# A new instruction order for the five engines in a block of sliding-window attention and gMLP on one core

## Chip, cores and metric

The kernel runs on one core of a Trainium2 chip. The time is device microseconds of one execution; the kernel before has a median of 277.32 us over three runs (277.1 to 277.49). One further execution of it was recorded by the profiler; it took 277.13 us.

## What is computed

One block on x of 2048 rows and 448 columns: attention over a window of 256 keys, then a gMLP whose spatial product mixes all 2048 rows, both behind a layer norm that is scaled and shifted by values from a conditioning vector c.

```python
mod = (silu(c) @ w_mod).reshape(1, 6, 1, 448)         # sa, ca, ga, sb, cb, gb
h = layernorm(x) * (1 + ca) + sa
q, k, v = split(h @ wqkv)                             # 16 heads of 28
p = softmax(where(0 <= i - j < 256, q @ k.T * 28**-0.5, -1e9))
x = x + ga * ((p @ v) @ wo)
h = layernorm(x) * (1 + cb) + sb
z = gelu(h @ w_in)                                    # 448 -> 1792
z1, z2 = z[:, :896], layernorm(z[:, 896:])
g = w_sp @ z2 + b_sp[:, None]                         # 2048 x 2048 times 2048 x 896
x = x + gb * ((z1 * g) @ w_out)
```

## The kernel before

**Tiles.** The 2048 rows are 16 tiles t0 to t15 of 128 rows, and four blocks tb0 to tb3 of four tiles. Everything stays in the on-chip memory; only x, the weights, two small rows of modulation values (`modrow`) and the result pass through DRAM.

**First norm and q, k, v.** DVE takes the statistics of x (L580, L583), POOL the inverse root (L585, L586), and DVE (L593) or POOL (L599) writes the normed tile `xn`. For tb0 and tb1 PE transposes it (L624, L712) and the modulation is applied as the banks are emptied into `hT` (L634/L635, L720/L722); for tb2 and tb3 a transposing DMA does it (L481, `hT<-xn`) and the modulation follows in place (L705/L707). The modulation values come from small products L537 with `w_mod`, one for each of four chunks of 128 rows. PE then forms q and k in eight groups g0 to g7 of four matmuls a block (L644 for tb0, L735 after it), which ACT or DVE copies out (L740/L741 q, L745/L746 k), and v by tile (L777; L781/L782). One more layout of q, `QBD`, is written by four small DMAs a block (L678).

**Attention.** Each tile j has two halves a and b of eight heads. I call the score group S(j)a, S(j)b. From tile 2 on such a group is 36 small matmuls (L879) into PSUM banks 0 to 3 and one matmul of 512 columns from `QBD` (L888, "Se") into bank 5. ACT takes the exponential of the four banks in one instruction of 128x2048 and of bank 5 in one of 128x512 (both L840). There is one set of banks 0 to 3, so S of a half cannot start until the exponential of the half before has read it. This gives a **ring**: score, exponential, next score; there are 28 such halves. DVE applies the masks (L895), PE multiplies with v (L922, bank 4), DVE divides (L936 reciprocal, L938) into `o_sb`, a transposing DMA (L481, `hT<-o_sb`) turns it, and PE multiplies with wo (L947). I call the last two oT(j) and mo(j). DVE adds x (L952), and the second norm and transposing DMA of the tile follow (`hT<-xn` again, from `xn2`), then its modulation (L970 ACT, L972 DVE or POOL).

**gMLP.** The two halves of w_in (L1032, L1053) are followed by gelu on ACT (L1039, L1061) and the norm of z on DVE (L1044). After that PE runs the spatial product L1077 in groups of 16 matmuls of 512 columns, DVE adds the bias (L1081), POOL multiplies with z1 (L1084), PE multiplies with w_out (L1094, L1102), DVE adds x (L1105, L1119) and SP sends the result. w_out is scaled by POOL (L963) before.

**Fillers.** At the start PE has little to do; matmuls on a tile of zeros (L550, one of 512 columns each) are put in there. The program defines 40 of them and emits those that the order names: 17.

**What sets the order.** Nothing decides at run time. A list of 1226 operations with their dependences is built, and the string `ORDER` (lines 22 to 74) names each as `n.engine.slot`: operation number, engine (p PE, a ACT, v DVE, g POOL, s SP for DMA issues) and the PSUM banks or buffers that it takes. Each engine executes its operations in the order in which the string names them, and waits on semaphores where one depends on another engine, so an engine whose next operation is not ready holds all behind it. `LAND_*` (lines 393 to 397) and `land=` (lines 424, 425) are expected landing times of loads; they go into `op.end`, which sorts only the order in which an instruction's several waits are written (`items = sorted(want.items(), key=lambda x: -x[1][1].end)`).

Of the kernel before, what the change touches and what calls it, by code (L numbers as in the profile page):

```python
# [19 lines left out]
57.v 0.a 3.a 26.v 1.s 2.s 4.s 34.g 23.v 24.v 27.v 43.a 5.s 35.g 6.s 36.g 58.p.0 59.p.0 60.p.0 44.p.0 7.s 139.v 40.g 50.a 32.g 8.s 137.v 37.g 140.v 9.s  # L20
25.v 138.v 143.v 141.g 38.g 10.s 145.v 142.g 146.v 28.v 144.v 45.a 11.s 46.a 147.g 149.v.0 148.g 151.v.1 12.s 61.p.0 62.p.0 63.p.0 64.p.0 65.p.0
66.p.0 67.p.0 68.p.0 69.p.0 70.p.0 150.p.2.3 152.p 13.s 153.v.2 52.p.1 53.p 71.p.0 54.p 155.v.3 14.s 55.p 154.p 29.v 156.p 15.s 16.s 56.v 133.a 157.v
21.s 134.v 158.a 159.v 72.p.0 73.p.0 74.p.0 191.p.4 17.s 171.p.5 135.g 186.p.6 160.v 18.s 161.p.0 136.a 172.p 162.p 192.p 49.g 176.p.1 163.p 47.a
177.p 196.p.2 166.p.3 42.g 193.p 41.g 164.p 213.v 167.p 165.a 173.p 178.p 215.v 168.p 48.a 174.p 51.v 179.p 214.v 217.v 197.p 169.p 175.a 219.v 187.p
198.p 170.a 199.p 39.v 181.p.0 180.a 188.p 218.v 220.v 194.p 216.v 200.v 189.p 221.g 195.a 182.p 222.g 183.p 30.v 184.p 190.a 374.p.0 185.v 205.p.1
375.a.0 229.g 225.g 211.s 227.g 223.g 122.p.0 228.v.0 226.g.1 212.s 201.p.6 224.v.2 19.s 230.g.3 123.v 206.a 380.p.0 125.s 202.v 231.p.0 381.a.1 210.s
234.p.1 232.v 124.s 235.v 399.p.0 233.a 203.p.6 209.s 236.v 400.a.2 269.v 251.p.0 31.v 271.v 401.a 243.p.1 376.v 265.v 126.s 252.a 406.p.0 267.v 127.s
407.a.3 241.p.0 244.v 270.v 266.v 268.v 239.p.1 272.v 204.v 408.a 273.g 274.g 242.v 377.p.0 240.a 402.v 426.p.0 378.v 237.p.0 279.g 427.a.4.0 382.v
277.g 319.v 33.g 428.p.0 281.g 280.v.0 379.p 263.p.1 275.g 320.v 282.v.1 285.s 276.g.2 321.v 238.a 434.p.0 384.v 278.g.3 247.p.0 264.v 435.a.5.1 283.s
409.v 383.p 129.g 249.p.1 248.v 284.s 322.v 411.v 385.p 429.a 455.p.0 131.g 250.v 245.p.0 456.a.6.2 386.v 323.v 286.s 132.g 387.v.0 207.p.1 325.v  # L30
403.p.0 256.s 457.p.0 246.v 208.a 463.p.0 458.a 253.s 404.v 259.p.1 464.a.0.3 438.v 255.s 439.v 405.p 410.p 388.s 261.p.0 430.v 431.v 412.p 262.a
484.p.0 254.s 413.v 287.v 436.p.0 485.a.1.4 414.v.1 257.p.0 459.v 432.p.0 288.v 433.p 290.v 440.p 258.v 437.a 492.p.0 289.v 260.a 465.p.0 489.v 441.p
493.a.2.0 295.p.0 326.v 460.v 442.v 305.p.1 488.v 466.a 324.v 443.v.2 327.g 513.p.0 296.a 328.g 468.v 444.s 515.p.0 514.a.3.1 461.p.0 467.v 462.p
291.p.0 335.g 497.v 415.s 130.g 306.v 469.p 516.a 521.p.0 292.v 329.g 470.p 522.a.4.2 331.g 336.v.0 297.p.1 333.g 332.v.1 330.g.2 471.v 472.v.0
486.p.0 445.p.0 496.v 473.s 487.a 542.p.0 298.a 446.v 494.p.0 543.a.5.3 490.p.0 447.v 22.s 389.p.1 334.v.3 337.s 526.v 491.p 303.p.0 390.v 495.a 517.v
338.s 550.p.0 304.a 525.v 301.p.1 551.a.6.4 546.v 339.s 391.v 293.p.0 518.v 498.p 302.a 340.s 554.v 552.p.0 499.p 294.a 571.p.0 500.v 553.a 501.v.2
474.p.1 310.s 572.a.0.0 307.s 299.p.0 475.v 309.s 476.v 523.p.0 519.p.0 502.s 524.a 555.v 520.p 300.a 579.p.0 448.v 547.v 317.p.1 580.a.1.1 341.g
308.s 477.v 527.p 576.v 528.p 311.p.0 478.g 342.v 479.g 392.v 318.a 529.v 344.v 573.p.0 530.v.1 480.g 600.p.0 574.a 343.g 312.v 416.p.1 531.s
601.a.2.2 449.g 584.v 544.p.0 503.p.0 450.g 417.v 20.s 393.g 575.v 548.p.0 545.a 608.p.0 504.v 549.p 418.v 556.p 609.a.3.3 505.v 315.p.1 419.v 420.g
557.p 451.g 394.g 349.p.0 558.v 605.v 316.a 421.g 581.p.0 583.v 629.p.0 582.a 559.v.0 345.p.1 630.a.4.4 506.v 604.v 560.s 577.p.0 507.g 346.v 395.g  # L40
578.p 452.g.0 602.p.0 585.p 350.a 508.g 633.v 637.p.0 603.a 586.p 509.g 396.v.1 638.a.5.0 351.p.1 481.g.2 453.v 422.g 587.v 454.s 612.v 610.p.0
347.p.0 588.v.2 352.a 642.v 658.p.0 611.a 589.s 606.p.0 348.v 659.a.6.1 561.p.1 613.v 128.s 660.p.0 397.v 641.v 607.p 398.s 614.p 423.g.0 562.v 661.a
666.p.0 482.v 615.p 662.v 667.a.0.2 313.p.0 355.s 634.v 483.s 631.p.0 563.v 532.p.1 616.v 564.v 314.a 617.v.1 565.g 687.p.0 510.g.1 632.a 533.v
# [223 lines left out]
def bass_adaLN_cond__sliding_block__mixer_gmlp__prompt_kernel(  # L267
# [13 lines left out]
    S, D, H, DH = 2048, 448, 16, 28  # L281
# [910 lines left out]
```

## Time and profile before

| | value |
|---|---|
| median of 3 runs | 277.32 us |
| profiled execution | 277.13 us |
| span in its profile, first to last instruction | 275.4 us |
| outside the span | 1.73 us |
| PE busy in the span | 265.9 us (97%) |
| DVE, ACT, POOL busy | 162.9, 128.2, 111.6 us |
| first exponential (of tile 0) starts | 19.49 us |
| first exponential of the ring, S(2)a, starts | 28.94 us |
| last score of the ring, S(15)b, starts | 104.36 us |
| first spatial product starts | 154.28 us |
| last product's result starts to be added | 272.16 us |

Times within the profile are counted from the start of the span. An engine's busy time counts each matmul from its start to its modelled end, and as matmuls overlap in the pipeline, a group of several takes longer by its row than the distance to the next group.

### The profile page before, as it was taken

What the parts mean: (1) busy time and instruction counts of PE and PEld (TensorE: products, weight loads), DVE (VectorE), ACT (ScalarE), POOL (GpSimd) and SP (SyncE); (2) the same over time, 40 slices, a digit from 0 to 9 for tenths busy, and PEclk for the clock granted to TensorE, in tenths of its full rate; (3) what the DMA queues carried; (4) which work ended last, traced back from release to release, by engine and by line L of the source; (5) the groups of instructions that cost most, each with busy time, mean ns of one, the idle gap of its engine ahead of it and who ended that gap; (6) DMA issues with size and microseconds to landing.
All of it is one profiled execution on the core that took longest, in us unless ns stands there. A gap on an engine that the chain in (4) does not pass through costs nothing.

```text
span 275.4 us, 7324 instructions
## 1 busy us (share of the span) xinstructions
PE 265.9 (97%) x3174; PEld 139.3 (51%) x3196; DVE 162.9 (59%) x365; ACT 128.2 (47%) x152; POOL 111.6 (41%) x185
## 2 busy tenths in 40 slices
PE   8898999998999999999999999999999999999995
PEld 2544566465667575544444444444444444454452
DVE  7578999997899899696799202110340300341543
ACT  3598899997999999847756500000000000000000
POOL 4440914126644714864549103140361730370400
PEclk9999999999999999999999999999999999999999
DMA  7995362457344777949699999000000000001123
GB/s 207 339 253 147 88 88 33 93 96 204 82 71 71 98 116 153 144 100 167 110 184 175 172 190 187 0 2 0 0 1 2 0 0 0 2 0 33 60 67 109
DMA packets 66862, 26.48 MB, mean 96 GB/s; under 512 B 57801, under 2 KB 65742, under 8 KB 66830
## 3 DMA queue, kind: packets, MB, share of 16 engines
q1 hardware_dynamic: 66748, 25.90, 46.1%
q8 instruction: 25, 0.41, 0.6%
q10 hardware_dynamic: 82, 0.12, 0.1%
q14 instruction: 7, 0.06, 0.1%
HBM read 9.47 MB, written 1.84 MB: 41 GB/s over the span
## 4 chain that ended last, share of the span: by engine, by line
PE 73%; DVE 11%; DMA 7%; ACT 4%; SPq 2%; POOL 1%; issue 1%
PE ps L1077 35%; PE ps L1032 8%; PE ps L1053 8%; PE ps L1094 7%; DMA hT<-o_sb 4%; ACT PW L840 4%; PE ps L947 4%; PE ps L922 3%; PE ps L879 3%; DVE st_all L580 3%; DMA x_sb<-in_A_x_dram 3%; DVE PT L895 2%; PE ps L777 1%; PE ps L764 1%; PE ps L735 1%
## 5 line engine op out<-in xcount | busy, mean ns | idle before, releaser
L840 ACT ACTIVATE PW<-ps 128x2048 bf16<-128x2048 f32 (+1 forms) x56 | 67.1, 1244 | 4.5 <-PE ps L879 1.8
L1081 DVE TENSOR_TENSOR tmpg<-ps,bsp_bc 128x512 bf16<-128x512 f32 x28 | 19.0, 689 | 74.6 <-PE ps L1077 64.6
L1084 POOL TENSOR_TENSOR z1T<-tmpg,z1T 128x512 bf16<-128x512 bf16 x28 | 31.7, 1151 | 73.7 <-DVE tmpg L1081 73.6
L1077 PE MATMUL ps<-wspB,z 128*128 128x512 bf16 x219 | 49.2, 379 | 0.3
L1077 PE MATMUL ps<-wspA,z 128*128 128x512 bf16 x219 | 48.7, 379 | 0.4 <-issue 0.2
L895 DVE TENSOR_TENSOR PT<-PW,mask 128x1024 bf16<-128x1024 bf16 x56 | 36.3, 673 | 0.7 <-ACT PW L840 0.7
L1077 PEld LDWEIGHTS ps<-wspA,z 128*128 128x128 bf16 x224 | 21.8, 98 | 26.6 <-DVE z L1044 0.4
L1077 PEld LDWEIGHTS ps<-wspB,z 128*128 128x128 bf16 x224 | 21.9, 98 | 26.3
L585 POOL TENSOR_SCALAR ve_all<-mv_all 128x1 f32<-128x1 f32 (+2 forms) x37 | 10.1, 280 | 48.3 <-DVE mv_all L583 47.8
L586 POOL TENSOR_TENSOR rs_all<-ve_all,neghalf 128x1 f32<-128x1 f32 (+2 forms) x37 | 26.2, 717 | 1.0
L922 PE MATMUL ps<-Vaug,PT 128*128 128x29 bf16 x496 | 24.8, 176 | 0.0
L922 PEld LDWEIGHTS ps<-Vaug,PT 128*128 128x128 bf16 x496 | 22.3, 96 | 4.4 <-DVE o_sb L938 0.9
L1032 PE MATMUL ps<-w_in,hT 64*128 64x448 bf16 x224 | 22.9, 349 | 0.0
L1053 PE MATMUL ps<-hT,w_in 64*128 64x512 bf16 x196 | 22.5, 376 | 0.0
L1094 PE MATMUL ps<-w_out_g,z1T 128*128 128x448 bf16 x105 | 20.7, 352 | 0.0
L922 PE MATMUL ps<-Vaug,PW 128*128 128x29 bf16 x224 | 20.4, 175 | 0.0
L580 DVE BATCH_NORM_STATS2 st_all<-x_sb 128x6 f32<-128x448 bf16 x32 | 18.9, 613 | 1.5 <-DMA x_sb<-in_A_x_dram 1.4
L580 DVE BATCH_NORM_STATS2 st_all<-z 128x6 f32<-128x448 bf16 x32 | 18.5, 605 | 2.1 <-ACT z L1039 2.0
L735 PE MATMUL ps<-hT,WQK 128*128 128x512 bf16 x69 | 17.8, 380 | 1.4 <-issue 0.3
L922 PEld LDWEIGHTS ps<-Vaug,PW 128*128 128x128 bf16 x224 | 17.7, 96 | 2.2
L1061 ACT ACTIVATE z1T<-ps 128x512 bf16<-128x512 f32 x28 | 14.8, 610 | 7.1 <-PE ps L1053 7.0
L1039 ACT ACTIVATE z<-ps 128x896 bf16<-128x896 f32 x16 | 14.1, 914 | 6.8 <-PE ps L1032 6.8
(112 smaller groups left out, 326.6 us busy)
## 6 DMA issues: line engine op xcount, KB each, us to landing
out_dram<-fin SPq DMA_DIRECT2D x15, 112.0 KB, 1.7
x_sb<-in_A_x_dram SPq DMA_DIRECT2D x3, 448.0 KB, 7.0
w_in<-in_B_w_in_dram SPq DMA_DIRECT2D x1, 1344.0 KB, 6.3
wmod<-in_w_mod_dram SPq DMA_DIRECT2D x1, 1296.0 KB, 10.8
QBD<-qT SPq DMA_DIRECT2D x16, 64.0 KB, 2.9
w_out_g<-in_B_w_out_dram SPq DMA_DIRECT2D x1, 784.0 KB, 5.8
wmod<-in_w_mod_dram SPq DMA_DIRECT2D x3, 240.0 KB, 5.6
wq_st<-in_A_wqkv_dram SPq DMA_DIRECT2D x3, 224.0 KB, 5.8
```

The source lines that it names most:

```text
L580: st = [dve(0.62 if True else 0, lambda e, t=t, ci=ci, s=s: e.bn_stats(st_all[:, slot, t, ci, :], s()), deps(t), prio) for ci, s in enumer ...
L586: rs = pool(0.53 + 0.15 * len(tiles), lambda e: e.tensor_tensor(rs_all[:, slot, a:b], ve_all[:, slot, a:b], neghalf[:, 0:b - a], ALU.pow), ...
L735: m = pe(4 * MMS, [lambda e, h=h, g=g, kc=kc, tb=tb: e.matmul(ps[:, h.slot[0], :], lhsT=WQK[:, kc, 4 * g:4 * g + 4, :].rearrange("p a b -> ...
L840: ex = act(xdur, lambda e, out_ap=out_ap, in_ap=in_ap: e.activation(out_ap(), in_ap(), ACT.Exp, scale=SCALE), [s], v - 8.0 + u, takes, tab ...
L895: return dve(0.70, lambda e: e.tensor_tensor(cols(hp.slot[0] * 2048 + 1024 * k, [[256, 4], [128, 2], [1, 128]]), cols(at_w() + 128 + 192 * ...
L922: fns.append(lambda e, hp=hp, hO=hO, hi=hi, bi=bi, kb=kb, hd=hd, nb=nb, a=at[hi][bi], p_of=p_of: e.matmul(ps[:, hO.slot[0], 32 * hd:32 * h ...
L1032: return lambda e, kc, p0, start, stop: e.matmul(ps[:, hs[t % 2].slot[hf], 0:D], lhsT=hT[p0:p0 + 64, kc, t * 128:(t + 1) * 128], rhs=w_in[ ...
L1053: return lambda e, kc, p0, start, stop: e.matmul(ps[:, hs[b // 2].slot[b % 2], :], lhsT=w_in[p0:p0 + 64, kc, ft * 128:(ft + 1) * 128], rhs ...
L1077: m = pe(16 * MMS, [lambda e, h=h, si=si, ft=ft, tb=tb: e.matmul(ps[:, h.slot[0], :], lhsT=z2[:, si, ft * 128:(ft + 1) * 128], rhs=(wspA i ...
L1081: a = dve(0.7, lambda e, h=h, ht=ht, tb=tb: e.tensor_tensor(tmpg[:, ht.slot[0], :], ps[:, h.slot[0], :], bsp_bc[:, tb * 512:(tb + 1) * 512 ...
L1084: u = pool(1.16, lambda e, ht=ht, ft=ft, tb=tb: e.tensor_tensor(z1T[tb][:, ft, :], tmpg[:, ht.slot[0], :], z1T[tb][:, ft, :], ALU.mult), [ ...
L1094: return [lambda e, ft=ft: e.matmul(ps[:, h.slot[0], 0:D], lhsT=z1T[t // 4][:, ft, (t % 4) * 128:(t % 4 + 1) * 128], rhs=w_out_g[:, ft, :] ...
```

## The change

`ORDER` is replaced, and the numbers for the expected landings with it. The operations are the same, but that one more filler is named (18 for 17, so 1181 words for 1180). 57 operations change their engine: 17 from DVE to ACT, 13 from ACT to DVE, 11 from POOL to DVE, 10 from DVE to POOL, 4 from ACT to POOL, 2 from POOL to ACT. The first line of the string, and the landing numbers:

```diff
-57.v 0.a 3.a 26.v 1.s 2.s 4.s 34.g 23.v 24.v 27.v 43.a 5.s 35.g 6.s 36.g 58.p.0 59.p.0 60.p.0 44.p.0 7.s 139.v 40.g 50.a 32.g 8.s 137.v 37.g 140.v 9.s
+57.v 0.a 3.a 23.v 1.s 34.g 26.v 49.a 2.s 4.s 35.g 24.v 27.v 5.s 6.s 36.g 25.v 58.p.0 59.p.0 60.p.0 44.p.0 28.v 38.g 7.s 137.v 45.a 40.g 8.s 139.v 32.g
...
-    LAND_M = (5.4, 6.5, 7.4, 8.1)
-    LAND_Q = (8.9, 9.6, 10.2, 10.7)
-    LAND_V = (11.6, 12.0, 12.9)
-    LAND_B = (16.8, 18.0)
-    LAND_L = (19.9, 20.9, 21.1, 22.3, None, None, None)
+    LAND_M = (6.4, 7.2, 8.2, 8.8)
+    LAND_Q = (9.3, 10.2, 11.0, 11.55)
+    LAND_V = (12.65, 12.95, 14.0)
+    LAND_B = (18.6, 19.5)
+    LAND_L = (21.0, 22.0, 22.3, 23.5, 33.0, 34.0, 34.5)
```

The expected landing of `d_x01` goes from 4.3 to 4.1 and that of `d_wq3` from 5.5 to 5.0 in the same way.

**Place 1: PE from q, k of tb1 to the first score of the ring.** The rows run from the second scores of tile 0 (L853, 8 matmuls) to S(2)a (L879); L712 transposes the normed tiles of tb1, L735 with x8 is two of the groups g, with x4 one. Before:

```order
L853 MATMUL ps<-qT,KT 128x128 x8
L712 MATMUL ps<-ident,xn 128x128 x16
L853 MATMUL ps<-qT,KT 128x128 x16
L664 MATMUL ps<-wv,hT 128x448 x4
L735 MATMUL ps<-hT,WQK 128x512 x8
L853 MATMUL ps<-qT,KT 128x128 x16
L735 MATMUL ps<-hT,WQK 128x512 x8
L922 MATMUL ps<-Vaug,PT 128x29 x4
L879 MATMUL ps<-qT,KT 128x128 x4
```

In the change:

```order
L853 MATMUL ps<-qT,KT 128x128 x8
L712 MATMUL ps<-ident,xn 128x128 x16
L853 MATMUL ps<-qT,KT 128x128 x16
L664 MATMUL ps<-wv,hT 128x448 x4
L888 MATMUL ps<-QBD,KT 128x512
L735 MATMUL ps<-hT,WQK 128x512 x4
L853 MATMUL ps<-qT,KT 128x128 x16
L735 MATMUL ps<-hT,WQK 128x512 x4
L922 MATMUL ps<-Vaug,PT 128x29 x8
L735 MATMUL ps<-hT,WQK 128x512 x4
L879 MATMUL ps<-qT,KT 128x128 x4
```

Three groups of q, k stand ahead of S(2)a where four stood; a second small group of products with v is ahead of it, and so is the first Se (L888), which needs the four `QBD` loads of tb0. Those four loads are issued by SP one behind the other where two other loads and `modrow` stood between them. Beside these rows, the four tiles `xn` of tb1 are all written by DVE where POOL wrote two, one of the four evacuations of `hT` goes from ACT to DVE, and one copy of k of tb1 too.

**Place 2: PE around S(6)a.** L947 is mo(2); the L879 rows are S(6)a; L735 is a group of q, k of tb2; the L888 behind it is an Se of an earlier half. Before:

```order
L735 MATMUL ps<-hT,WQK 128x512 x4
L888 MATMUL ps<-QBD,KT 128x512
L947 MATMUL ps<-wo_g,hT 128x448 x4
L879 MATMUL ps<-qT,KT 128x128 x4
L879 MATMUL ps<-qT,KT 128x64 x16
```

In the change:

```order
L735 MATMUL ps<-hT,WQK 128x512 x4
L888 MATMUL ps<-QBD,KT 128x512
L735 MATMUL ps<-hT,WQK 128x512 x4
L879 MATMUL ps<-qT,KT 128x128 x4
L879 MATMUL ps<-qT,KT 128x64 x16
L879 MATMUL ps<-qT,KT 64x64 x16
L947 MATMUL ps<-wo_g,hT 128x448 x4
```

mo(2) stands behind the score, and another group of q, k ahead of it.

**Place 3: SP around oT(4).** `hT<-xn` x4 are the transposes of the normed tiles of tb3, `QBD` x3 are three of the four loads of q of tb2, and the first `hT<-o_sb` behind them is oT(4), the next one oT(5). Before:

```order
L481 DMA_TRANSPOSE hT<-xn 128x4x128 x4
L678 DMA QBD<-qT 32x2x512 x3
L481 DMA_TRANSPOSE hT<-o_sb 128x4x128
L678 DMA QBD<-qT 32x2x512
L481 DMA_TRANSPOSE hT<-o_sb 128x4x128
```

In the change the first `hT<-o_sb` shown is oT(3), the second oT(4):

```order
L481 DMA_TRANSPOSE hT<-xn 128x4x128 x2
L481 DMA_TRANSPOSE hT<-o_sb 128x4x128
L567 DMA modT<-modrow 128x8x1
L481 DMA_TRANSPOSE hT<-xn 128x4x128
L481 DMA_TRANSPOSE hT<-o_sb 128x4x128
L678 DMA QBD<-qT 32x2x512 x4
```

oT(4) is ahead of all four loads of q of tb2, and the transposes of tb3 are spread between oT(0) and oT(4). On PE mo(4) stands behind S(8)a as before, but mo(1), which stood between the two, is earlier.

More of the change, by code (lines that the diff above doesn't have):

```diff
@@ L24 @@
[L24 to L43, printed above, removed]
@@ L75 @@
+1181.p.4 1217.v.0 1213.v.1 1218.s 1214.s 1182.v.3 1183.s
 """
```

91 lines of the change are left out of this document (55 added, 36 removed).

## Prediction

> **What bounds the kernel now.** I read the page's totals first, then busy time by stretch, the two lists of waits, and last the timeline of PE and ACT at the places that the waits name.
>
> ```profile
> span 275.4 us, 7324 instructions
> PE 265.9 (97%) x3174; PEld 139.3 (51%) x3196; DVE 162.9 (59%) x365; ACT 128.2 (47%) x152; POOL 111.6 (41%) x185
> ```
>
> PE is busy for 97% of the span, so the end is set by PE: the work that it has, and the moments when it has none. The stretches tell where those are (length, then PE busy, PEld, DVE, ACT, POOL, granted clock, DMA share, GB/s; the clock is 1.00 in each):
>
> ```profile
> 18.20:28.90 10.70, 9.73 (x139) 4.75 (x140) 9.05 (x23) 9.60 (x11) 4.25 (x9) 1.00 0.71 170
> 28.90:45.00 16.10, 15.63 (x353) 9.28 (x355) 16.10 (x40) 15.34 (x16) 6.88 (x13) 1.00 0.37 60
> 60.00:75.00 15.00, 13.98 (x339) 8.55 (x339) 12.60 (x30) 13.18 (x14) 10.93 (x19) 1.00 0.55 145
> 109.70:122.00 12.30, 12.30 (x156) 6.46 (x154) 9.52 (x23) 8.15 (x10) 9.78 (x18) 1.00 0.80 126
> 154.30:240.60 86.30, 85.89 (x392) 39.13 (x400) 14.23 (x21) 2.59 (x6) 24.43 (x22) 1.00 0.20 38
> ```
>
> From 109.7 on PE has next to no hole. The spatial products and the last sum and store keep their form and their order of kinds in the change, so I take 154.3 to 275.4 as a block that is shifted whole. What the change can move lies before. In the ring of attention the holes are small by this measure (0.47 of 16.10 at first, 1.02 of 15.00 in 60 to 75), but overlapping matmuls hide part of the wait in them; the ring is better read by its steps:
>
> ```profile
> 28.94 1.88 ACT L840 ACTIVATE PW<-ps 128x2048 bf16<-128x2048 f32 x1
> 30.72 0.59 ACT L740 ACTIVATE qT<-ps 128x512 bf16<-128x512 f32 x1
> 31.53 1.88 ACT L840 ACTIVATE PW<-ps 128x2048 bf16<-128x2048 f32 x1 [0.22 <-PE ps L879]
> ```
>
> One exponential starts 2.59 after the other, and ACT stood idle for 0.22 before the second because the score was not there. A step is thus at least 2.59: exponential 1.88, and 0.71 from its end through the next score. It is longer where PE has more than that to do between two scores, or ACT more between two exponentials, or where PE stands. From S(2)a (28.29) to S(15)b (104.36) there are 27 steps; 27 times 2.59 is 69.9 of the 76.07 recorded. I worked all 27 through, always carrying the later of three times on: the exponential before, PE's groups between the scores, ACT's instructions between the exponentials. PE's prices are distances between starts:
>
> ```profile
> 62.21 0.55 PE L879 MATMUL ps<-qT,KT 32*128 32x128 bf16 x36
> 62.69 0.93 PE L947 MATMUL ps<-wo_g,hT 128*128 128x448 bf16 x4
> 63.45 0.38 PE L888 MATMUL ps<-QBD,KT 128*128 128x512 bf16 x1
> 66.86 1.88 ACT L840 ACTIVATE PW<-ps 128x2048 bf16<-128x2048 f32 x1 [1.63 <-PE ps L922]
> 68.63 0.54 ACT L781 ACTIVATE Vaug<-ps 128x448 bf16<-128x448 f32 x1
> ```
>
> A score costs 0.48, an mo 0.76 (a v product of the same form the same). On ACT the next starts 0.11 before the row's end (66.86 + 1.88 = 68.74, next at 68.63), so an exponential counts 1.77, a copy of 0.54 counts 0.43, of 0.60 about 0.49. The result for the kernel before is S(15)b at 102.75, where 104.36 was recorded. The 1.61 missing fall almost whole on two steps:
>
> ```profile
> PE ps L947 <- DMA hT<-o_sb: 1.3, 3, 0.9
> 49.27 0.93 PE L947 MATMUL ps<-wo_g,hT 128*128 128x448 bf16 x4 [0.25 <-DMA hT<-o_sb]
> 64.72 0.93 PE L947 MATMUL ps<-wo_g,hT 128*128 128x448 bf16 x4 [0.89 <-DMA hT<-o_sb]
> 105.99 0.93 PE L947 MATMUL ps<-wo_g,hT 128*128 128x448 bf16 x4 [0.15 <-DMA hT<-o_sb]
> ```
>
> mo(2) at 49.27 makes S(6)a late by 0.43, and mo(4) at 64.72 makes S(8)b late by 1.05; the ACT row above has the second one's mark, 1.63 idle. The third, mo(12), is behind the last score. Their transposes in the chain that ended last:
>
> ```profile
> 45.10 4.12 DMA hT<-o_sb
> 60.47 4.20 DMA hT<-o_sb
> 102.55 3.39 DMA hT<-o_sb
> ```
>
> **The change, part by part.**
>
> *The two stalls: -1.5.* mo(2) goes behind S(6)a. It would reach PE some 1.3 later (one group of q, k and a score), past the landing at 45.10 + 4.12 = 49.22, so the score no longer waits for it. For mo(4) the cause is SP:
>
> ```profile
> 56.73 0.62 DVE L938 TENSOR_TENSOR o_sb<-ps,rec_all 128x448 bf16<-128x448 f32 x1
> 58.00 2.42 SPq L678 DMA_DIRECT2D QBD<-qT  x3
> 60.47 1.28 SPq L481 DMA_TRANSPOSE hT<-o_sb  x1
> ```
>
> The tile was ready at 57.35 and its transpose was issued at 60.47, behind three loads of q. Ahead of them it can go out up to 2.4 earlier, and even at 4.20 it lands before mo(4) is reached. Those loads then go out some 1.3 later; PE's first use of them is several steps off. I take both stalls as gone: 0.43 + 1.05 = 1.5 (1.6 with the small remainder).
>
> *The ring's other steps: +1.4.* Here the new order is less even. The same walk over its order, from the same start, takes 75.83 instead of 74.46, which is +1.37. PE has 0.83 more work between the first and the last score: the group of q, k that no longer stands ahead of S(2)a (0.86) and the first products with v of tile 14 (0.29) have come in, an Se (0.22) and a small group (0.10) have gone out ahead of it. And in some steps ACT has two copies beside its two exponentials, 1.77 + 0.43 + 0.43 + 0.49 = 3.12, or a modulation:
>
> ```profile
> L840 ACT ACTIVATE PW<-ps 128x512 bf16<-128x512 f32 x28 | 16.9, 604 | 0.7 <-PE ps L888 0.3
> L781 ACT ACTIVATE Vaug<-ps 128x448 bf16<-128x448 f32 x8 | 4.3, 542 | 0.1
> L970 ACT ACTIVATE hT<-hT,modT 128x512 bf16<-128x512 bf16 x5 | 3.8, 804 | 1.0 <-DMA hT<-xn 1.0
> ```
>
> The modulation counts 0.69, so such a step is 1.77 + 0.69 + 0.49 = 2.95 (priced by L970; L705 has no row on ACT in this trace). DVE, which has no free moment in 28.9 to 45 (16.10 of 16.10), has the same load there up to the quotients of tiles 1 to 3 (+0.06, +0.08 and 0.00 by the class means), 0.9 less up to that of tile 0 and 2.2 less up to tile 4, so I add nothing for it.
>
> [...]
>
> *The start of the ring: -0.6 (between -1.1 and +0.2).*
>
> ```profile
> 19.64 1.65 POOL L599 TENSOR_SCALAR xn<-x_sb,rs_all,ve_all 128x448 bf16<-128x448 bf16 x2
> 21.43 1.05 PE L712 MATMUL ps<-ident,xn 128*128 128x128 bf16 x16 [0.24 <-POOL xn L599]
> 22.08 1.58 DVE L722 TENSOR_SCALAR hT<-ps,modT 128x512 bf16<-128x512 bf16 x3 [0.45 <-PE ps L712]
> 23.94 1.67 PE L735 MATMUL ps<-hT,WQK 128*128 128x512 bf16 x7 [0.26 <-DVE hT L722]
> 25.95 1.04 PE L735 MATMUL ps<-hT,WQK 128*128 128x512 bf16 x4
> 27.23 1.04 PE L735 MATMUL ps<-hT,WQK 128*128 128x512 bf16 x4 [0.24 <-DVE qT L741]
> 28.29 0.55 PE L879 MATMUL ps<-qT,KT 32*128 32x128 bf16 x36
> ```
>
> The two tiles of POOL end at 21.29; on DVE (0.43 each) all four are done about 0.4 earlier, but DVE then has four instead of three copies of hT, so hT of tb1 is complete at 23.6 as before (23.66). Behind it four groups of q, k stood ahead of S(2)a, now three. One group is 0.86 (four matmuls of 512 at 0.215), the extra products and Se cost 0.1 and 0.22 ahead of it. If all of it counts, S(2)a starts 1.1 earlier; if the exponentials of tile 1 hold it, only 0.2. DVE must deliver a copy of k more in the same time, which could cost 0.2 net. I take the middle of the first two, -0.6. The filler (0.215) lies in front of q, k of tb0, where PE waits for hT anyway.
>
> *Behind the ring: -0.7 (between -1.1 and -0.3).* The products with v of tile 14 that went into the ring are 0.29 less behind S(15)b. Two waits stand there: mo(12), 0.31 to its reach at 105.99, and
>
> ```profile
> PEld ps L1077 <- DVE z L1044: 0.4, 1, 0.4
> 154.28 1.03 PE L1077 MATMUL ps<-wspA,z 128*128 128x512 bf16 x4 [0.16 <-issue]
> ```
>
> 0.53 before the first spatial product. With tile 15's products up to 1.4 nearer to the last score the new order can lose either or keep both; I take half of 0.84.
>
> *A wait that is new: +0.3 (between 0 and +1.1).* Several mo have a new place; the three recorded ones cost 0.31, 0.43 and 1.05. One small one is likelier than none. mo(9), only some 5.4 behind its product with v, is the nearest candidate: 0.25 and 0.62 on DVE and 4.2 for the DMA come to 5.1.
>
> The sum: -1.5 + 1.4 - 0.6 - 0.7 + 0.3 = -1.1, with the remainder of the walk (1.61 for 1.48) -1.2. The profiled execution of 277.13 (span 275.4 and 1.73 around it) becomes 275.9; the median of the runs shown is 0.19 above it, so the forecast is 276.1.
>
> **Rivals.**
>
> *A, the stalls' time is given back.* The ring takes 1.37 more and 1.5 less; if S(2)a gains only 0.2 and both late waits stay, the sum is -1.5 + 1.4 - 0.2 - 0.3 + 0.3 = -0.3: 277.0. For it: the first two are near equal. Against it: that a group less stands ahead of S(2)a is in the order, and the ring's 1.37 has that group in it already, so a start that gains nothing would pay for it twice.
>
> *B, slower, by the first Se.* PE executes in order, and Se of S(2)a now stands ahead of the first group of q, k of tb1. It needs all four loads of q of tb0.
>
> ```profile
> 18.69 1.40 SPq L678 DMA_DIRECT2D QBD<-qT  x2
> 22.74 0.59 SPq L678 DMA_DIRECT2D QBD<-qT  x1
> DMA to landing us min/median/max: 2.0/2.9/4.6
> ```
>
> Before, the last was issued at 22.74 and nothing ahead of 29.4 needed it. In the new order they go out together, the last at about 19.9, and land at 22.8 with the median and at 24.5 with the longest. PE could begin q, k at 23.6. Up to a landing at 23.4 it costs nothing, then each 0.1 costs 0.1; at 24.5 it is 0.9 plus the Se. If a copy of q before them is late by 1 more, S(2)a starts 0.8 later than before instead of 0.6 earlier, and the sum is +0.3 or, with a second stall of mo(9)'s kind at 0.43, +0.7: 278.0. For it: DMA is 0.71 busy in that stretch. Against it: SP has little else to issue there.
>
> *C, a transposing DMA is not slow.* In the trace a transpose of one tile took 4.12, 4.20 and 3.39 where PE waited; a load of q took 2.9 in the median. Were these 1.3 a passing crowd, each mo would have 1.3 more air and the walk would hold without a new wait and with mo(12) gone: -1.2 - 0.3 - 0.4 = -1.9, 275.4. [...]
>
> *D, nothing moves.* The landing numbers alone change no instruction, only the order of waits; the order rows show that the rest does move PE's groups, so that I give this no chance of its own.
>
> **Numbers.** A measurement of this kernel tells apart about 0.2%, or 0.55 us: faster is below 276.77, slower above 277.87. The forecast 0.49, its own range 274.9 to 276.8; A 0.22, of it 0.04 faster, 0.16 within and 0.02 slower; B 0.19, of it 0.03 within and 0.16 slower; C 0.10, all faster. The ends of the range are the sums of the ends: lowest -1.5 + 1.4 - 1.1 - 1.1 - 0.1 = -2.4, 274.9; highest is B at 278.0. Faster is 0.49 + 0.04 + 0.10 = 0.63, same 0.16 + 0.03 = 0.19, slower 0.18.
>
> **What would show it.** Right: no wait of L947 at S(6)a and S(8)b, no ACT idle of 1.6 there; S(2)a at 27.2 to 28.1; S(15)b at 103 to 104, with steps of 2.9 to 3.2 where ACT has two copies or a modulation; first spatial product near 153.1. Wrong: a wait of PE for `QBD` ahead of L735 near 24, a wait of L947 at another tile, a wait of L1032 for POOL (w_out's scaling stands ahead of a modulation there), or steps over 3.2.

## The result, and the profile after

The changed kernel takes 281.45 us in the median of four runs (281.23 to 282.11), where the kernel before took 277.21 beside it. The ratio is 1.0164, with a 95% interval of 1.0132 to 1.0197. It is slower by 4.2 in the medians and by some 4.5 by the ratio, and 276.1 with a range of 274.9 to 278.0 was forecast. In a later sitting the same kernel gave a ratio of 1.0145 (1.0117 to 1.0173). The profiled execution took 282.11, with a span of 280.4.

The page's first lines and, behind them, three of the stretches that the prediction shows (length, PE busy, PEld, DVE, ACT, POOL, granted clock, DMA share, GB/s):

```profile
span 280.4 us, 7322 instructions
PE 267.7 (95%) x3175; PEld 140.5 (50%) x3197; DVE 163.0 (58%) x362; ACT 130.4 (47%) x155; POOL 110.0 (39%) x186
PEclk9999959999999999999999999999999999999999
```

```profile
18.20:28.90 10.70, 9.92 (x144) 4.91 (x145) 10.49 (x28) 9.74 (x11) 0.77 (x3) 1.00 0.58 148
28.90:45.00 16.10, 12.47 (x217) 6.82 (x218) 10.98 (x27) 10.72 (x13) 7.06 (x11) 0.79 0.49 123
60.00:75.00 15.00, 13.76 (x322) 8.49 (x323) 13.30 (x30) 13.93 (x15) 7.97 (x14) 1.00 0.28 48
```

Nearly all of it stands in one stretch. In 28.9 to 45 PE is busy for 12.47 of 16.10, where it was 15.63; DVE falls from 16.10 to 10.98 and ACT from 15.34 to 10.72; and the clock is 0.79, with a 5 in the sixth slice of the page's clock. In 18.2 to 28.9 POOL is busy for 0.77 only, where it was 4.25. That is the trail to follow. PE's list of waits names the place:

```profile
PE ps L664 <- DVE KT L746: 3.1, 1, 3.1
...
PE ps L947 <- DVE x_sb L952: 0.8, 1, 0.8
PE ps L1077 <- DVE z L1044: 0.7, 1, 0.7
...
PE ps L888 <- DMA QBD<-qT: 0.3, 1, 0.3
```

The chain that ended last shows what stood behind that copy of k (start, duration, what):

```profile
21.26 2.26 DMA modrow<-rows
23.54 6.07 DMA gg_sb<-modrow
29.68 2.04 POOL wo_g L569 x2
31.82 0.25 POOL ve_all L585
32.13 1.05 POOL rs_all L586
33.27 0.27 POOL ve_all L597
33.57 0.40 DVE xn L593
...
35.37 0.59 DVE KT L746
36.01 1.68 PE ps L664 x4
```

Two scalings of wo (L569) stand on POOL ahead of the norm of tb2 in the new order. They wait for `gg_sb`, a row that comes back from DRAM, and it landed 6.07 after its issue. POOL waited, and behind it the norm of tb2; behind the norm DVE waited; behind DVE's norm stood a copy of k, and behind that copy's bank a product on PE. Before, the scalings stood behind the norm (L585 to L599 on POOL), and both copies of `gg_sb` landed within 3.3:

```profile
27.55 0.23 POOL L585 TENSOR_SCALAR ve_all<-mv_all 128x4 f32<-128x4 f32 x1 [6.26 <-DVE mv_all L583]
32.33 3.39 POOL L569 TENSOR_TENSOR wo_g<-wo_g,gg_sb 128x448 bf16<-128x448 bf16 x3
```

```profile
DMA to landing us min/median/max: 3.1/3.2/3.3
```

In the change, the rows on SP and POOL, and on PE from S(3)a (32.33) to S(3)b (40.17):

```profile
23.54 0.35 SPq L566 DMA_DIRECT2D gg_sb<-modrow  x1
23.93 0.43 SPq L408 DMA_DIRECT2D w_in<-in_B_w_in_dram  x1
```

```profile
29.68 2.04 POOL L569 TENSOR_TENSOR wo_g<-wo_g,gg_sb 128x448 bf16<-128x448 bf16 x2 [10.72 <-DMA gg_sb<-modrow]
```

```profile
32.33 0.55 PE L879 MATMUL ps<-qT,KT 32*128 32x128 bf16 x36
36.01 1.68 PE L664 MATMUL ps<-wv,hT 128*128 128x448 bf16 x4 [3.13 <-DVE KT L746]
37.90 1.49 PE L735 MATMUL ps<-hT,WQK 128*128 128x512 bf16 x3 [0.22 <-issue]
40.17 0.77 PE L879 MATMUL ps<-qT,KT 32*128 32x128 bf16 x36
```

The four v matmuls took 1.68 instead of 0.93, and the score 0.77 instead of 0.55: PE came out of its stand at half the clock.

```profile
36.00:38.00 2.00, 1.77 (x5) 0.83 (x7) 1.97 (x5) 0.00 (x0) 1.23 (x2) 0.50 0.47 70
```

### The profile page after: what moved, and what is told of

It reads as the page before. It is cut to its first block, busy times and chain, and to the rows that moved or that the text cites. A ratio compares the mean times of both kernels' runs of the same rounds, so it can differ in the third digit from the quotient of the medians.

```text
span 280.4 us, 7322 instructions
## 1 busy us (share of the span) xinstructions
PE 267.7 (95%) x3175; PEld 140.5 (50%) x3197; DVE 163.0 (58%) x362; ACT 130.4 (47%) x155; POOL 110.0 (39%) x186
## 3 DMA queue, kind: packets, MB, share of 16 engines
HBM read 9.47 MB, written 1.84 MB: 40 GB/s over the span
## 4 chain that ended last, share of the span: by engine, by line
PE 65%; DVE 17%; ACT 7%; DMA 4%; POOL 4%; issue 2%; DVEq 0%
PE ps L1077 34%; PE ps L1094 7%; PE ps L1032 6%; ACT PW L840 5%; DVE PT L895 5%; DVE st_all L580 3%; PE ps L644 2%; PE ps L922 2%; DMA gg_sb<-modrow 2%; PE ps L1053 2%; POOL rs_all L586 2%; DVE z L1044 2%; PE ps L550 2%; PE ps L947 2%; PE ps L777 2%
## 5 line engine op out<-in xcount | busy, mean ns | idle before, releaser
L585 POOL TENSOR_SCALAR ve_all<-mv_all 128x1 f32<-128x1 f32 (+2 forms) x37 | 10.0, 276 | 49.4 <-DVE mv_all L583 48.9
L586 POOL TENSOR_TENSOR rs_all<-ve_all,neghalf 128x1 f32<-128x1 f32 (+2 forms) x37 | 23.8, 662 | 1.0
L580 DVE BATCH_NORM_STATS2 st_all<-z 128x6 f32<-128x448 bf16 x32 | 18.1, 603 | 3.8 <-ACT z L1039 3.8
L580 DVE BATCH_NORM_STATS2 st_all<-x_sb 128x6 f32<-128x448 bf16 x32 | 18.8, 612 | 1.2 <-DMA x_sb<-in_A_x_dram 1.1
L735 PE MATMUL ps<-hT,WQK 128*128 128x512 bf16 x69 | 18.5, 390 | 1.0 <-issue 0.2
```

The costliest lines, as they stand in the source:

```text
L580: st = [dve(0.62 if True else 0, lambda e, t=t, ci=ci, s=s: e.bn_stats(st_all[:, slot, t, ci, :], s()), deps(t), prio) for ci, s in enumer ...
L586: rs = pool(0.53 + 0.15 * len(tiles), lambda e: e.tensor_tensor(rs_all[:, slot, a:b], ve_all[:, slot, a:b], neghalf[:, 0:b - a], ALU.pow), ...
L735: m = pe(4 * MMS, [lambda e, h=h, g=g, kc=kc, tb=tb: e.matmul(ps[:, h.slot[0], :], lhsT=WQK[:, kc, 4 * g:4 * g + 4, :].rearrange("p a b -> ...
```

## The experiments

How the steps stand in each kernel is read from the start of the scores; e1 to e12 are the runs below in short. Starts in their profiled executions, in us (a difference of two can be off by 0.01 through rounding):

| score | before | change | e1 | e6 | e7 | e5 | e9 | e12 |
|---|---|---|---|---|---|---|---|---|
| S(2)a | 28.29 | 27.16 | 27.13 | 26.98 | 26.80 | 27.87 | 28.13 | 26.89 |
| S(3)a | 33.46 | 32.33 | 32.30 | 32.15 | 31.97 | 33.08 | 33.30 | 33.54 |
| S(3)b | 36.17 | 40.17 | 35.12 | 34.97 | 35.16 | 35.83 | 35.92 | 36.77 |
| S(5)a | 44.38 | 49.36 | 45.05 | 43.70 | 44.34 | 44.04 | 44.09 | 44.98 |
| S(6)a | 50.13 | 55.50 | 51.20 | 49.84 | 50.48 | 49.26 | 49.76 | 50.66 |
| S(8)a | 62.21 | 67.74 | 63.39 | 61.18 | 61.82 | 62.09 | 61.83 | 62.73 |
| S(8)b | 65.87 | 70.34 | 66.00 | 63.79 | 64.43 | 64.70 | 64.44 | 65.67 |
| S(15)b | 104.36 | 109.42 | 105.08 | 102.87 | 103.51 | 103.45 | 103.38 | 104.26 |
| span | 275.4 | 280.4 | 276.0 | 273.8 | 274.5 | 274.7 | 274.0 | 275.4 |

Runs of one kernel here spread by more than the first three of the kernel before did: beside e5 to e8 that kernel gave 275.4 to 279.2, and the intervals of the ratios below are 0.22% to 0.88% to either side, where the prediction counted on 0.2%. A profile is one execution as well. With the order before, S(2)a starts at 28.29, 28.13, 27.87 and, in e8, at 27.40. The distance between two scores repeats far better: S(7)a to S(7)b takes 3.01 in every profile. So differences under 1 us are read below from such steps, and where neither a step nor the medians decide, the text says so.

**e1: the two scalings go back behind the norm.** Rows of POOL:

```diff
 L500 MEMSET o_sb 128x3x64
-L569 TENSOR_TENSOR wo_g<-wo_g,gg_sb 128x448 x2
 L585 TENSOR_SCALAR ve_all<-mv_all 128x4
...
 L599 TENSOR_SCALAR xn<-x_sb,rs_all,ve_all 128x448
-L569 TENSOR_TENSOR wo_g<-wo_g,gg_sb 128x448
+L569 TENSOR_TENSOR wo_g<-wo_g,gg_sb 128x448 x3
```

> The changed kernel, with the two scalings of wo (L569) on POOL moved behind the norm of tb2, where the kernel before has them; nothing else. Theory P (POOL stands for gg_sb with these two, and the norm of tb2, a copy of k on DVE and a v product on PE stand behind it): POOL begins the statistics of tb2 at 27.6 in place of 31.8, the wait of L664 for the copy of k (3.1) goes, the clock stays at 1.00 in 32 to 43, and the time falls by about 5.0 to 276.4 (between 275.8 and 277.0). Rival R (DVE has too much to do in 28 to 36, as the change gave it two norms and a copy more; POOL is only the releaser named last): L664 still waits over 1 us and the time stays above 279.

Measured: 276.63, ratio 0.9984 (0.9951 to 1.0017). POOL begins the norm of tb2 as soon as DVE has its sums, PE no longer stands, and the clock is 1.00 from 28.9 to 46.5:

```profile
27.75 0.30 POOL L585 TENSOR_SCALAR ve_all<-mv_all 128x4 f32<-128x4 f32 x1 [8.38 <-DVE mv_all L583]
```

```profile
32.30 0.55 PE L879 MATMUL ps<-qT,KT 32*128 32x128 bf16 x36
32.78 0.93 PE L664 MATMUL ps<-wv,hT 128*128 128x448 bf16 x4
```

With two instructions on POOL put back, no slowdown is left that the interval could tell from nothing. The rival, too much work on DVE, would have left a wait of L664.

**e2: the place stays, the load of w_in moves.** Rows of SP:

```diff
 L566 DMA gg_sb<-modrow 128x448
-L408 DMA w_in<-in_B_w_in_dram 128x3x1792
 L565 DMA modrow<-rows_68 2x64
...
 L481 DMA_TRANSPOSE hT<-o_sb 128x4x128 x2
+L408 DMA w_in<-in_B_w_in_dram 128x3x1792
```

> The changed kernel, with the load of w_in (1344 KB) moved on SP from right behind gg_sb to where the kernel before has it, behind oT(5); POOL keeps its order. Theory Q (the place on POOL hurts only because gg_sb shares the DMA engines with w_in): gg_sb lands 3.2 after its issue, at 26.8 in place of 29.6, POOL begins the statistics of tb2 at 28.9 in place of 31.8, L664 waits under 0.4 in place of 3.1, and the time falls by 4 to 5 to 277 (276.4 to 277.6). If the latency comes from elsewhere (the x load ahead of it, the row written to DRAM just before): gg_sb still takes over 5, and the time stays within 0.7 of 281.4.

Measured: 277.98, ratio 1.0040 (1.0005 to 1.0075). The time is 0.4 above the range that was expected, 276.4 to 277.6. The row lands earlier, POOL begins at 27.39, and of the wait of 3.13 on PE 1.01 is left:

```profile
27.39 2.23 POOL L569 TENSOR_TENSOR wo_g<-wo_g,gg_sb 128x448 bf16<-128x448 bf16 x2 [8.12 <-DMA gg_sb<-modrow]
```

```profile
33.90 0.93 PE L664 MATMUL ps<-wv,hT 128*128 128x448 bf16 x4 [1.01 <-DVE KT L746]
```

The copy of `gg_sb` that POOL waits for landed after 4.0 here, after 6.1 in the change. So both theories hold, as two factors of one stall: the place makes POOL wait for the row, and the 1344 KB of w_in, issued 0.4 behind it, make the row late. More of the wait is left than expected, since POOL reached the norm at 29.7 and not at 28.9. Why the copy took 4.0 and not the 3.2 of the kernel before is open.

**e3: the kernel before, with the two scalings ahead of the norm.**

```diff
 L599 TENSOR_SCALAR xn<-x_sb,rs_all,ve_all 128x448 x2
+L569 TENSOR_TENSOR wo_g<-wo_g,gg_sb 128x448 x2
 L585 TENSOR_SCALAR ve_all<-mv_all 128x4
...
-L569 TENSOR_TENSOR wo_g<-wo_g,gg_sb 128x448 x3
+L569 TENSOR_TENSOR wo_g<-wo_g,gg_sb 128x448
```

> The kernel before, with the two scalings of wo moved ahead of the statistics of tb2 on POOL; nothing else. There gg_sb is issued at 25.6 and lands at about 28.9, so POOL would begin the statistics of tb2 at 31.0 in place of 27.6. Theory P: DVE stands at the norm of tile 8 (30.0 before) until about 33, the copies of k behind it and PE's groups behind them are late by some 3, the clock falls as PE stands, and the time rises by 2.5 to 5, to 280 to 282. Rival R (the place does nothing without the rest of the change): within 0.6 of 277.2.

Measured: 279.92, ratio 1.0103 (1.0016 to 1.0191), in a wide spread (278.58 to 282.24). The mechanism comes with the place alone; the large load of w_in goes out far later in this kernel, at 66.6:

```profile
27.82 2.22 POOL L569 TENSOR_TENSOR wo_g<-wo_g,gg_sb 128x448 bf16<-128x448 bf16 x2 [6.93 <-DMA gg_sb<-modrow]
```

```profile
34.50 1.04 PE L735 MATMUL ps<-hT,WQK 128*128 128x512 bf16 x4 [1.54 <-DVE Vaug L782]
```

S(3)a is 2.10 later than in the kernel before, and the profiled execution, at 278.58, is the fastest of the four. After a stand of 1.54 its clock is still 1.00. Over its four executions of 278.58, 278.73, 281.10 and 282.24 the mean clock is 0.999, 0.999, 0.994 and 0.986. DVE waits only 0.8 for the norm here; two masks (L915) that run beside the scalings take 1.05 and 1.26 where they took 0.42 before, and that is a second part of the delay (e6 takes it up).

**e4: fillers in the stall.** Rows of PE in the change:

```diff
 L879 MATMUL ps<-qT,KT 64x64 x16
+L550 MATMUL ps<-wz 128x512 x14
 L664 MATMUL ps<-wv,hT 128x448 x4
```

> The changed kernel, with 14 more fillers (L550, 0.215 each, 3.0 together) on PE right ahead of the v product that stands for 3.1; nothing else. If the cost of the stall is the wait of 3.1 and besides about 1.9 that PE needs more because its granted clock is 0.50 from 35.4 to 41.5: the clock stays at 1.00, the step from S(3)a to S(3)b falls from 7.8 to about 6, and the time falls by 1.5 to 2.0 to 279.6. If the lower clock costs nothing (the steps behind are held by ACT and DVE): within 0.5 of 281.4.

Measured: 280.36, ratio 1.0105 (1.0028 to 1.0182).

```profile
33.49 3.19 PE L550 MATMUL ps<-wz 128*128 128x512 bf16 x14 [0.84 <-ACT KT L745]
36.52 0.92 PE L664 MATMUL ps<-wv,hT 128*128 128x448 bf16 x4
38.84 0.55 PE L879 MATMUL ps<-qT,KT 32*128 32x128 bf16 x36
```

```profile
36.00:38.00 2.00, 1.95 (x11) 0.95 (x10) 2.00 (x5) 0.00 (x0) 0.89 (x1) 1.00 0.37 68
```

The clock stays at 1.00. From the v product to S(3)b PE now needs 38.84 - 36.52 = 2.32, where the change needed 40.17 - 36.01 = 4.16. In e1, which has no stand there, it is 35.12 - 32.78 = 2.34. The clock's share of the stall is thus 1.84. Only 1.1 of it is seen in the step (6.74 for 7.84), as the fillers themselves waited 0.84 and then held PE to the start of the v product at 36.52, 0.5 later than in the change. In the second profiled execution of the change (e11) the lower clock ended earlier: the step took 7.46 (31.96 to 39.42), so that e4 gains 0.7 on it. The clock answers the question, the time does not: the interval of e4 takes in that of e11, 1.0117 to 1.0173.

**e6: the masks beside POOL.** e1 still lost time from 35 to 45 that the walk did not know. Its masks L915 were slow while POOL scaled wo:

```profile
32.19 3.42 POOL L569 TENSOR_TENSOR wo_g<-wo_g,gg_sb 128x448 bf16<-128x448 bf16 x3
```

```profile
33.97 1.92 DVE L915 TENSOR_TENSOR PT<-PT,mask 128x512 bf16<-128x512 bf16 x2
```

The edit to e1 at line 569, which leaves out most of the scaling:

```diff
-e.tensor_tensor(wo_g[:, kc, :], wo_g[:, kc, :], gg_sb[:, 0, :], ALU.mult)
+e.tensor_tensor(wo_g[:, kc, 0:8], wo_g[:, kc, 0:8], gg_sb[:, 0, 0:8], ALU.mult)
```

> As e1_scale_late, but the four scalings of wo (L569) cover 8 of 448 columns, so that the rest of wo stays unscaled. It asks why e1 loses 1.1 between 35 and 42 where the walk had it 1.2 ahead of the kernel before at S(3)b. Theory S: DVE's masks L915 take 0.96 in place of 0.41 there because POOL runs L569 at the same time (32.2 to 35.6). Then the pair at 34.0 takes 0.8 in place of 1.92, the copy of v (L669) is 1.1 earlier, PE's waits there (0.37 for that copy, 0.85 for L936 at 43) shrink, and the time falls by 0.5 to 1.0 against e1. If DVE is merely overloaded: the pair keeps about 0.96 each, and the time is within 0.3 of e1.

Measured: 276.25, ratio 0.9966 (0.9939 to 0.9992).

```profile
31.86 0.52 POOL L569 TENSOR_TENSOR wo_g<-wo_g,gg_sb 128x8 bf16<-128x8 bf16 x3
```

```profile
33.78 0.74 DVE L915 TENSOR_TENSOR PT<-PT,mask 128x512 bf16<-128x512 bf16 x2
```

The pair takes 0.74 for 1.92, and S(5)a comes 1.35 earlier than in e1, 1.2 of it behind S(2)a. The medians, of two sittings, differ by 0.4. That lies between the two expectations, 0.5 to 1.0 and under 0.3, so the masks' rows decide here and not the time. In this kernel the ring takes 102.87 - 26.98 = 75.89; the walk of the prediction gave 75.83.

**e7: two moves on DVE.** Rows of DVE, against e1:

```diff
+L669 CAST Vaug<-ps 128x16x28
 L915 TENSOR_TENSOR PT<-PT,mask_60 128x4x128 x2
...
-L669 CAST Vaug<-ps 128x16x28
...
+L952 TENSOR_TENSOR x_sb<-ps,x_sb 128x448
 L707 TENSOR_SCALAR hT<-hT,modT 128x512
-L952 TENSOR_TENSOR x_sb<-ps,x_sb 128x448
```

> As e1_scale_late, with two moves on DVE: the sum of x of mo(1) (L952) ahead of the modulation that waits 1.54 for a transpose (L707), and the copy of v of tile 3 (L669) ahead of the two masks L915. The first takes away the wait of 0.78 of the next mo at 61, the second the wait of 0.37 at 37. If these waits lie on the path, S(8)a is 0.8 earlier against e1, S(4)a 0.3, and the time falls by 0.8 to 1.1, to about 275.6. If the ring takes it back (S(8)b is held by ACT's modulation step), less than 0.3.

Measured: 276.36, ratio 0.9970 (0.9947 to 0.9992). In the change DVE stood at a modulation for a transpose, with the sum of mo(1) behind it, and mo(3), which needs that sum's bank, waited on PE:

```profile
64.31 0.41 DVE L707 TENSOR_SCALAR hT<-hT,modT 128x512 bf16<-128x512 bf16 x1 [1.59 <-DMA hT<-xn]
64.63 0.62 DVE L952 TENSOR_TENSOR x_sb<-ps,x_sb 128x448 bf16<-128x448 f32 x1
```

```profile
65.31 0.93 PE L947 MATMUL ps<-wo_g,hT 128*128 128x448 bf16 x4 [0.83 <-DVE x_sb L952]
```

With the order turned round, the step to S(8)a is 2.9 (58.92 to 61.82) where e1 had 3.8. But e6 has it at 2.9 too (58.27 to 61.18), without this move: its L707, at 56.97, does not wait. So the wait comes with a late transpose, and the move is one way round it. S(15)b is 1.6 earlier than in e1 and the span 1.5 shorter, but the median, of another sitting, only 0.3, less than the 0.8 to 1.1 that was expected; the profiled execution of e1 (277.75) was the slowest of its ten, 1.1 above their median.

**e5 and e9: the two stalls of the kernel before.** e9 moves oT(4) on SP alone, e5 mo(2) on PE as well:

```diff
-L678 DMA QBD<-qT 32x2x512 x3
 L481 DMA_TRANSPOSE hT<-o_sb 128x4x128
-L678 DMA QBD<-qT 32x2x512
+L678 DMA QBD<-qT 32x2x512 x4
...
-L947 MATMUL ps<-wo_g,hT 128x448 x4
 L879 MATMUL ps<-qT,KT 128x128 x4
 L879 MATMUL ps<-qT,KT 128x64 x16
 L879 MATMUL ps<-qT,KT 64x64 x16
+L947 MATMUL ps<-wo_g,hT 128x448 x4
```

> The kernel before with two moves alone: oT(4) on SP ahead of the three loads of q of tb2, and mo(2) on PE behind S(6)a. By the prediction's first term both stalls go (0.43 and 1.05 in the ring) and the time falls by 1.5, to about 275.3 beside 276.8 (ratio 0.9945). Rival: what is gained is lost at the next place that was just in time (the loads of q of tb2 land some 1.3 later, DVE stands behind mo), and less than 0.5 is left.

> The kernel before with oT(4) alone ahead of the loads of q of tb2; mo(2) stays ahead of S(6)a. In e5 the move of mo(2) gained 0.52 at S(6)a and lost 0.75 at S(6)b, where PE then had 2.91 + 0.76 = 3.67 between two scores. If so, without it: S(6)a keeps its wait of 0.4, S(6)b loses nothing, S(8)b is 1.05 earlier against its own start, and the time falls by 0.6 to 1.0 against the kernel before, as much as e5 or 0.2 more. If the gain of oT(4) is itself given back (e5 lost 0.37 at S(10)a), under 0.5.

Measured: e5 276.32, ratio 0.9973 (0.9947 to 1.0000); e9 275.75, ratio 0.9972 (0.9949 to 0.9995). oT(4) is worth what was forecast at its place: the step to S(8)b is 1.06 shorter, and then 0.47 is given back at S(10)a. Behind S(15)b e9 is 0.38 shorter than the kernel before (170.67 for 171.05), but e8 and e3, without the move, have 170.66 there, so this cannot be put down to the move. The move of mo(2) shows no gain: e5's ratio is about that of e9. PE reaches S(6)a 0.45 earlier against S(2)a, now held by ACT, and has mo(2), mo(0) and a group of q, k before S(6)b:

```profile
49.26 0.55 PE L879 MATMUL ps<-qT,KT 32*128 32x128 bf16 x36 [0.59 <-ACT PW L840]
49.74 0.93 PE L947 MATMUL ps<-wo_g,hT 128*128 128x448 bf16 x4
...
51.03 0.92 PE L947 MATMUL ps<-wo_g,hT 128*128 128x448 bf16 x4
...
53.04 0.55 PE L879 MATMUL ps<-qT,KT 32*128 32x128 bf16 x36
```

That step is 3.78 for 3.02. A stall that is moved into a step with work of its own is still paid for.

**e8: the landing numbers alone**, put into the kernel before.

```diff
-    LAND_M = (5.4, 6.5, 7.4, 8.1)
+    LAND_M = (6.4, 7.2, 8.2, 8.8)
...
```

> The kernel before with the new landing numbers alone and its own order: only the sequence of waits at five instructions differs. Expected: no change, within 0.2% of the kernel before. If the sequence of waits cost something, the start up to the first score would be later.

Measured: 276.37, ratio 0.9985 (0.9957 to 1.0012). They do nothing that can be measured in the time. The ring takes 76.07, as before. S(2)a starts at 27.40, 0.89 earlier than in the kernel before, and most of that is there already at q, k of tb0 (L644 at 10.38 for 11.06); e3, e5 and e9, with the old numbers, begin these at 10.76, 10.60 and 10.15. That is the spread of the start, and not shown to come from the numbers.

**e10: the old order behind the ring**, from the first Se of tile 15 of e7. The first of PE's rows that differ:

```diff
 L888 MATMUL ps<-QBD,KT 128x512
-L1032 MATMUL ps<-w_in,hT 128x448 x16
-L922 MATMUL ps<-Vaug,PT 128x29
...
-L1032 MATMUL ps<-w_in,hT 128x448 x40
+L1032 MATMUL ps<-w_in,hT 128x448 x22
...
```

> As e7_fix_dve up to the first Se of tile 15 (L888 behind S(15)b), and from there the order and the engines of the kernel before. It asks whether the order behind the ring costs something: in the change PE stands 0.90 ahead of the second group of spatial products for a norm of z (L1044), in the kernel before 0.31 at the first. If that is the whole difference there, the time falls by 0.4 to 0.6 against e7, to about 275.8 beside 277.0 for the kernel before (ratio 0.995). If the earlier end of the ring is lost to POOL or a transpose in the old order, it is as e7 or slower.

Measured: 280.28, ratio 1.0129 (1.0096 to 1.0163).

```profile
114.23 3.06 PE L1032 MATMUL ps<-w_in,hT 64*128 64x448 bf16 x16 [2.48 <-ACT hT L970]
```

```profile
110.00:116.00 6.00, 3.52 (x59) 1.91 (x57) 3.23 (x8) 4.72 (x6) 2.78 (x4) 0.80 0.94 189
```

At the seam a modulation waits for a transpose that the old order reaches too late. This does not answer what the order behind the ring costs; it only shows a second stand, of 2.48, during which the clock fell.

**e11: the change again.**

> The changed kernel again, so that it, e1 and e4 can be set against runs of the kernel before in the same sitting. Expected: the stall of 3.1 at L664 and a granted clock of 0.50 behind it in the profile, and a ratio of 1.013 to 1.020. If the stall depends on how late gg_sb happens to land, the executions spread by more than 1.

Measured: 280.59, ratio 1.0145 (1.0117 to 1.0173), in a spread of 0.86 (280.07 to 280.93). The stall is 3.2 again, with `gg_sb` 6.3 to its landing: it belongs to the order, not to one execution.

**e12: the start of the change and oT(4).** The kernel before, with e9's move, and the order and engines of the change up to S(2)a, but the scalings and w_in; its rows on PE are those of place 1. One small load of w_in (L409), which the kernel before issues at 8.94, goes out at 23.99 here.

```diff
-L735 MATMUL ps<-hT,WQK 128x512 x8
+L888 MATMUL ps<-QBD,KT 128x512
+L735 MATMUL ps<-hT,WQK 128x512 x4
...
```

> The kernel before with oT(4) ahead of the loads of q of tb2 (e9), and with the start of the changed order, its engines too, up to S(2)a; the two scalings of wo and the load of w_in stay where the kernel before has them, and from S(2)a on all follows the order before. Of the change it keeps the two parts that the runs showed to gain: the start (S(2)a 1.1 to 1.5 earlier) and oT(4) (1.05). PE then has one group of q, k more behind S(2)a (0.86), which stretches one step of the ring past 2.6. If the start's gain stays but for some 0.4 of that: 0.7 less than e9, ratio 0.9945. If the ring takes it back whole: the ratio of e9, 0.997. If DVE or POOL stands again at the seam: slower than e9.

Measured: 277.47, ratio 1.0028 (1.0000 to 1.0057). S(2)a starts at 26.89, 1.40 earlier than in the kernel before, and S(2)b at 30.92, not earlier at all:

```profile
26.89 0.55 PE L879 MATMUL ps<-qT,KT 32*128 32x128 bf16 x36 [0.15 <-ACT PT L840]
27.37 1.04 PE L735 MATMUL ps<-hT,WQK 128*128 128x512 bf16 x4
29.19 1.04 PE L735 MATMUL ps<-hT,WQK 128*128 128x512 bf16 x4 [0.79 <-DVE qT L741]
```

The group of q, k that no longer stood ahead of S(2)a stands behind it, and one more wait of 0.79 with it.

## Why the prediction was wrong

The step that failed is "a wait that is new: +0.3 (between 0 and +1.1)". It was sized by the three recorded waits of mo, and looked for only there. The new wait was on POOL, for a row from DRAM, and e1 against the change in the profiled executions puts its price at S(3)b at 40.17 - 35.12 = 5.05: 3.2 of standing and 1.84 of lower clock. (By the step from S(3)a, against e1's 2.81, it is 5.03 in this execution and 4.65 in e11.) Another step had closed the way to it. Of DVE I said that it "has the same load there", and so added nothing; that sum was of durations, and a DVE that waits for POOL has the same load. And of POOL I named a place behind the ring and none at its start. That the scalings had gone ahead of a norm, onto a transfer with a large load issued right behind it, could be read from the order and from the landing of 3.2 for `gg_sb` before.

The other terms, by the spans (280.4 - 275.4 = 5.0):

- *Start of the ring, -0.6:* right in direction and cause. S(2)a is 1.13 earlier, at the end of the range, and 1.16 to 1.5 in e1, e6 and e7. But against e8's 27.40 with the order before, the 1.13 would be 0.24. What the order gives is better read from the first group of q, k of tb1 to S(2)a: 4.35 to 4.57 in the five profiles with the old start, 3.33 to 3.75 in the nine with the new one, which is 0.6 to 1.2. The end of 1.1 was not worked out: the parts named there, 0.86 less 0.1 and 0.22, come to 0.54. The first Se waited only 0.3 for its loads, so rival B's place was not the one.
- *The two stalls, -1.5:* right in the change, where neither mo(2) nor mo(4) waits for a transpose any more, and S(8)a to S(8)b takes 2.61 for 3.67. e5 shows that the 0.43 of mo(2) could not be booked by itself.
- *The ring's other steps, +1.4:* the walk was right as far as it went. e6, which has neither the stall nor the slow masks and no wait of mo(3), takes 75.89 for the walk's 75.83. It is one execution, so that so close a match is in part luck. What the walk lacked is 2.05 more in e1 (105.08 - 27.13 = 77.95): some 0.8 of mo(3), and 1.2 from DVE's masks. As e1's profile is 1.1 above its median, part of this may belong to that execution alone. In the change itself the ring takes 82.26, of which the stall is 82.26 - 77.95 = 4.31, since PE, being late, did not meet a wait of 0.85 that e1 has at 43.
- *Behind the ring, -0.7:* wrong by that much. The products of w_in came in 0.66 earlier against S(15)b (the 91st of them starts at 124.64 for 120.24, 4.40 later, where S(15)b is 5.06 later), but PE then stood for a norm of z where I let a wait go:

```profile
159.27 1.03 PE L1077 MATMUL ps<-wspA,z 128*128 128x512 bf16 x4 [0.75 <-DVE z L1044]
```

From S(15)b to the end of the span it is the same within 0.1 (170.94 for 171.05); the order before has 170.66 to 171.27 there, execution by execution. The sum: -1.13 for the start, +1.88 for e1's ring (77.95 for 76.07), +4.31 for the stall and -0.1 behind it give the 5.0. The stall is the large term in any case; how the small ones share the rest rests on one profile each.

Rival A described e1, the change without its stall: the ratio 0.9984 is within the bound of no change. What decided lay outside all four rivals: B, too, was slower, but by another wait. No run tests C by itself. The three transposes that it went by are those that PE waited for; over all transposes into `hT` in the same trace the median landing is 3.4 (2.4 to 6.4), beside 2.9 (2.0 to 4.6) for loads of q of half the size, so those rows say little of transposes as such. Two versions are a little faster than the kernel before, e9 by 0.28% (0.05 to 0.51) and e7 by 0.30% (0.08 to 0.53).

## What to carry to other kernels

When a fixed order of several engines is changed, walk each engine down to its first instruction that waits for a transfer, and ask what is queued behind it there and, through the engines that wait for those, on the critical engine; sums of work by engine do not show such a wait. Price the wait with the transfers that are issued around the awaited one in the new order (6.07 to the landing here), not with its old landing (3.2). And a long stand of the matmul engine can cost more than its length, here 1.84 on top of 3.2. Filling it kept the clock but gained 0.7 to 1.1 in the step (e4); taking the cause away gained all of it (e1).

## What the runs showed of the hardware

**The clock after a stand.** PE's granted clock was 0.50 behind a stand of 3.13 (the change) and of 3.2 (e11), and 0.80 over a stretch with one of 2.48 (e10). Behind stands of 1.01 (e2) and 1.54 (e3) it stayed at 1.00 in the profiled executions, and in e4 with fillers in the gap as well. By the clock records of the traces it fell while PE still stood: in the change 1.9 after the end of the last matmul ahead of the stand, in e11 2.7 and in e10 1.9 after it. It then stayed at 0.50 for 6.83, 3.41 and 3.41. So how long it stays low differs between two executions of the change:

```profile
38.00:40.20 2.20, 2.20 (x24) 1.06 (x27) 2.20 (x6) 0.78 (x2) 0.00 (x0) 0.50 0.43 90
```

```profile
38.00:40.20 2.20, 2.20 (x58) 1.45 (x57) 2.20 (x6) 1.21 (x3) 0.00 (x0) 0.87 0.43 89
```

The first row is that of the run first shown, the second that of e11. Of these stands those of 2.48 and more had the lower clock behind them and those of 1.54 and less had not; from what length on it falls is not shown.

**DVE and POOL at once.** A mask L915 of 128x512 took 0.39 to 0.43 with no product L569 of POOL beside it (the change, the kernel before, e3), in e6 too (0.41), where POOL's products, cut to 8 columns, were over before. In e1 three masks began while POOL ran its products of 128x448, and took 0.45, 0.73 and 1.26. They ended at 33.51, 34.70 and 35.89, each 0.28 after the end of the product that was running (33.23, 34.42 and 35.61). None ended before the product that it met: begun 0.17, 0.45 and 0.98 ahead of that product's end, it took 0.28 more than that. By what mechanism is not shown. Beside the same products of POOL the cast L669 from PSUM took 0.62 (e7) and the sums L580 0.61 (e1, e7); in e6, with POOL done, both took 0.62.

**Transfers.** The copy of 224 KB from a DRAM row landed 3.1 to 3.3 after its issue in the kernel before, 3.1 to 3.5 in e3 and e9, and 4.0 in e2. With a load of 1344 KB issued 0.4 behind it, it landed after 6.1 and 6.3 in the two executions of the change, and after 5.7 in e1.
